# The second phase's order comes from twenty search passes with new prices, and the products by place load 128 columns

## The chip, the cores and the metric

The kernel runs on one core of a Trainium2 chip, as one launch. The metric is the time of one execution on the device in microseconds (us); three executions of the kernel before took 1140.48 to 1142.51 us, median 1141.89. A core has a matrix engine (PE, with its weight loads shown apart as PEld), a vector engine (DVE), an activation engine (ACT), a third elementwise engine (POOL), and SP, which here only issues transfers. Each engine works through its own list of instructions in the order in which they were written, and waits for the others at semaphores.

## The reference

Three layers follow one another. The kernel computes all of them, on 2304 tokens of 512 numbers:

```python
# 1. attention, 4 x 8 heads, 576 rows of 64: only the 32 largest scores of a row are kept
scores = scale * np.matmul(q, k.transpose(0, 1, 3, 2))
kth = np.partition(scores, -top_k, axis=-1)[..., -top_k:-top_k + 1]
scores = np.where(scores >= kth, scores, -1000000000.0)
attn = np.exp(scores - np.max(scores, axis=-1, keepdims=True))
x = (attn / (np.sum(attn, axis=-1, keepdims=True) + 1e-09)) @ v      # -> 2304 x 512
# 2. a dense layer, 512 -> 2048 -> 512
h = x @ w_in
x = np.where(h >= 1, h, np.where(h <= -1, 0.0, (h + 1) ** 2 / 4)) @ w_out
# 3. eight experts; each token goes to one, each expert takes 288 tokens at most
order = np.argsort(-(x @ w_gate).flatten())
for idx in order:                       # best pairs (token, expert) first
    tok, e = idx // E, idx % E
    if assigned[tok] < 0 and counts[e] < 288:
        assigned[tok] = e; counts[e] += 1
for e in range(8):
    out[assigned == e] = np.maximum(x[assigned == e] @ w1[e], 0) @ w2[e]
```

## The kernel before, in words

The program has two phases. The first does attention and the dense layer in blocks of 256 tokens; its last dense block is left half done for the second phase. The second phase does the rest of that block, the routing and the eight experts. This change touches the second phase alone.

No instruction is issued where it is written. Every call of an engine is recorded by a helper (`_Recorder.rec`, which is why nearly all rows of the profile name one line, L267, and are told apart by their tiles), with a price in nanoseconds, the tiles it reads and writes, and a rank. At the end of a phase `Program.issue` puts the recorded steps of all engines into one order and writes them out. `_pass` is a list scheduler: it plays the five engines through time and gives each engine, whenever it is free, the ready step with the smallest key. In pass 0 the key is the rank, which the author of the kernel wrote by hand (10 for each expert, with offsets such as `R_EX` and `R_XP`). Each further pass plays the steps backwards from their ends and takes the starts found there as new keys. `issue` keeps the order whose modelled end is earliest. Before, the first phase makes 10 further passes (`ROUNDS`), the second none (`ROUNDS_R = 0`): its order is the one by hand-written ranks.

What the second phase is made of, with the names that rows and order pieces use:

- **Routing** (`route`), eight rounds, one for each expert that fills up. Each has three search steps on DVE and PE: DVE writes `I` (128 x 2304 comparisons, in halves of 10 and 8 blocks), PE sums them into `pQ` by 18 small bf16 products (`pQ<-C,I`), DVE makes `ge`, PE spreads it (`pPT<-ge`), DVE takes `n0` and the next `y`, `yb`. From the third step come the expert's number `ei` and the tokens taken, counted through `SC` and a product into `pS` (`pS<-SC`).
- **Places** (`places`): DVE writes `oh`, a one-hot row of 96 for each token, and PE multiplies it by `Bt` in 18 small bf16 products (`pS<-Bt,oh`, weights `oh`); DVE reads off `idx`, the token numbers of the expert's 288 rows.
- **Gather** (`gathers`): three indirect transfers by POOL bring the rows `xg` out of `x2d` (the layer-2 output in DRAM).
- **The last dense block** (`last_block`): 96 products of 512 columns into `pX0` and `pX1`, copied by ACT into `yo` and stored to `x2d` by SP (`dram_x<-yo`); its rows for expert 0 are added by products with `taken` (`pH<-s,yo` and so on). The stores overwrite zero rows that the first gather reads, so they wait for it.
- **Expert** (`expert`): SP reads `ei` into a register and fetches eight pieces of the expert's weights, 512 KB each, into four buffers `raw` (four of w1, then four of w2). ACT rounds each to `W` (1024 columns), DVE writes the rest to another `W`. PE transposes `xg`, ACT and DVE split the result into two `XB`, and 192 products of 288 columns follow, 96 into `pH0`/`pH1` and 96 into `pX0`/`pX1` (`pH<-XB,W`, `pX<-XB,W`). Then transposes, `yo`, and three indirect stores by POOL. Since SP is one list, expert 0's w2 pieces stand behind the store `dram_x<-yo`.
- **Looks** (`look`, `totals`): 32 transfers of 512 KB into `s1`, each with two ACT passes (`size`), check the weights' range; `totals` turns them into a flag, read by all engines at the very end.

Of the kernel before, what the change touches and what calls it, by code (L numbers as in the profile page):

```python
# [11 lines left out]
BF16 = mybir.dt.bfloat16  # L12
# [28 lines left out]
R_QL, R_QS, R_QK, R_MK, R_PV, R_K, R_F, R_U = -4.0, -2.0, -1.2, 0.5, 1.0, 1.0, 1.5, 0.9  # L41
R_LB, SLOW, R_EX, R_XP, SPLIT_DVE, SPLIT_DVE0 = 12.0, 1.0, 25.0, -12.0, tuple(range(8)), tuple(range(8))
LATX, LATR, GRP = 1.5, 1.0, 1
ROUNDS, ROUNDS_R = 10, 0
X_DVE, H_DVE = True, tuple(range(8))
DEC0, GATE_H = 32, 0
WT_RAW, HALF, GD = False, 1.95, 1
# [165 lines left out]
class _Recorder:  # L213
# [5 lines left out]
    def __getattr__(self, method):  # L219
        def rec(*args, **kw):  # L220
            P, eng = self._prog, self._eng
            reads, writes = [], []
            for i, a in enumerate(args):
                if hasattr(a, "ap"):
                    (reads if i else writes).append(a)
            for k, a in kw.items():
                if hasattr(a, "ap"):
                    (writes if k in self.OUT else reads).append(a)
            if method == "matmul" and not kw["start"]:
                reads.append(writes[0])  # L230
            n = max(_free(a) for a in (writes[:1] if eng == "tensor" else reads + writes))
            inp = any(a.tensor.space == bass.MemoryType.PSUM for a in reads if hasattr(a.tensor, "space"))
            lat = None
            if eng == "vector":
                cost = 69 + 1.04 * n
                if method == "match_replace":
                    cost += 64
                if method == "tensor_scalar" and not inp:
                    cost = 69 + 0.52 * n
                if method == "scalar_tensor_tensor" and not inp:  # L240
                    cost = 69 + (1.04 if kw["in1"].dtype == I32 else 1.2) * n
                if method in ("tensor_tensor", "tensor_copy") and all(
                        x.dtype == BF16 and list(x.ap)[-1][0] == 1 for x in reads + writes):
                    cost = 69 + 0.52 * n
            elif eng == "scalar":
                cost = (51 if inp else 187) + 0.833 * n
                if not inp and args[2] in (AF.Copy, AF.Abs):
                    cost -= 93
                if "accum_out" in kw:
                    cost += 93  # L250
            elif eng == "gpsimd":
                cost = 148 + 2.1 * n
            elif eng == "sync":
                cost = max(60, 128 * min(_free(a) for a in reads + writes) * 4 / 360.0)
                lat = 2000 + 128 * min(_free(a) for a in reads + writes) * 4 / 180.0
            elif method == "transpose":
                cost = 109
            else:
                f32 = args[1].dtype == F32
                if args[1].dtype == F32R:  # L260
                    cost = 10 + 0.43 * n
                else:
                    cost = 2 * max(107, n * 2 / 2.4) + 1 if f32 else max(36, n / 2.4 + 3, 0.5 * _free(args[1]))
                if f32 and args[1].shape[-1] <= 64:
                    cost *= 0.63
            fn = getattr(getattr(P.nc, eng), method)
            P.add(eng, lambda: fn(*args, **kw), cost, reads, writes, lat)  # L267
        return rec


def _free(ap):
    n = 1
    for x in list(ap.shape)[1:]:
        n *= x
    return n
# [3 lines left out]
def kernel(ctx: ExitStack, tc: tile.TileContext, qm, qt, kT, vm, vt,  # L279
# [7 lines left out]
    pS = psum.tile([128, 2, 512], F32, name="pS")  # L287
# [8 lines left out]
    x2d = dram.tile([N, DM], F32, name="dram_x2")  # L296
# [550 lines left out]
    def second_phase(exact, rctx):  # L847
        rpool = rctx.enter_context(tc.tile_pool(name="rpool" + "x" * exact, bufs=1))
        P = Program(nc, LATR, True)
        V, A, G, T, Y = P.vector, P.scalar, P.gpsimd, P.tensor, P.sync  # L850
# [12 lines left out]
        def rt(shape, dt, tag, bufs=2):  # L863
            if tag not in rings:
                rings[tag] = Ring(tag, bufs, shape, dt)
            return rings[tag]()

        if exact:
# [3 lines left out]
            views, n = const_views(c1[:, 576:])  # L872
# [313 lines left out]
        def places(ph, ei, pos):  # L1186
            g1 = rt([128, NT], F32, "g1")
            V.tensor_scalar(g1, pos, 96.5, None, op0=ALU.is_ge)
            gq = rt([128, NT], BF16, "gq")
            V.scalar_tensor_tensor(out=gq, in0=pos, scalar=192.5, in1=g1, op0=ALU.is_ge, op1=ALU.add)  # L1190
            rr = rt([128, NT, 8], BF16, "rr8")
            V.scalar_tensor_tensor(out=rr, in0=bc(gq, [128, NT, 8], 2), scalar=-96.0, in1=bc(pos, [128, NT, 8], 2),
                                   op0=ALU.mult, op1=ALU.add)
            Bm = rt([128, 3, NT], BF16, "Bm")
            V.tensor_tensor(out=Bm, in0=bc(gq, [128, 3, NT], 1), in1=third, op=ALU.is_equal)
            Bt = rt([128, 2, 3, NT], BF16, "Bt")
            V.tensor_tensor(out=Bt, in0=bc(Bm, [128, 2, 3, NT], 1), in1=bc(tokb, [128, 2, 3, NT], 2), op=ALU.mult)
            for x, (ta, tb) in enumerate(HT):
                oh = rt([128, tb - ta, 96], BF16, f"oh{x}", 1)
                V.tensor_tensor(out=oh.rearrange("p t (g x) -> p t g x", x=8),  # L1200
                                in0=bc(rr[:, ta:tb], [128, tb - ta, 12, 8], 2),
                                in1=numbers(place96, tb - ta), op=ALU.is_equal)
                with P.group():
                    for t in range(ta, tb):
                        T.matmul(pS[:96, 1, :6], oh[:, t - ta, :], Bt.rearrange("p a g t -> p (a g) t")[:, :, t],
                                 start=(t == 0), stop=(t == NT - 1))
            idx = rt([96, 3], I32, "idx", 4)
            V.tensor_reduce(out=idx, in_=pS[:96, 1, :6].rearrange("p (a g) -> p g a", a=2), axis=AX, op=ALU.add)
            RES[ph] = (ei, idx)
# [31 lines left out]
        def gathers(ph):  # L1241
            idx = RES[ph][1]
            xg = XG[ph] = rt([96, 3, DM], F32, "xg", 2)

            def gather(g):
                return nc.gpsimd.indirect_dma_start(out=xg[:, g, :], out_offset=None, in_=x2d[:, :],  # L1246
                                                    in_offset=bass.IndirectOffsetOnAxis(ap=idx[:, g:g + 1], axis=0))

            P.rank -= 3.0
            for g in range(3):  # L1250
                P.add("gpsimd", partial(gather, g), 1000, [idx[:, g:g + 1], x2d[:, :]], [xg[:, g, :]], 3000)
            P.rank += 3.0

        def expert(ph):
            ei, idx = RES[ph]
            xg = XG[ph]
# [15 lines left out]
            hi, lo = [], []  # L1272
            for i in range(8):
                raw = rt([128, 1024], F32, "raw", 3 if exact else 4)
                P.add("sync", partial(fetch, raw, i // 4, i % 4), 1450, [ei[0:1, 0:1]] + [xg] * (early and i > 3), [raw], 2500)
                if i % 2 == 0:
                    wh, wl = W[wat[0] % 12], W[(wat[0] + 1) % 12]
                    wat[0] += 2
# [177 lines left out]
```

## Time and profile before

| | before |
|---|---|
| median of 3 executions | 1141.89 us |
| profiled execution, whole | 1138.19 us |
| profiled execution, first to last instruction (span) | 1136.3 us |
| PE busy in the span | 1051.2 us (93%) |
| DVE, ACT, POOL busy | 925.3, 808.9, 697.8 us |

The profiled execution is one run with the hardware profiler on; its own time is 1.9 us more than its span, and 3.7 us less than the median of the unprofiled ones. In the rows below, times are microseconds from the start of the span. In a timeline row, the numbers are start and length, and the brackets at its end say how long the engine stood idle before it and who released it. PEclk is the granted clock of PE: 1.00 is 2.4 GHz, 0.50 is 1.2 GHz.

### The profile page before, as it was taken

The numbers are of one execution on the slowest core, as the hardware profiler recorded it, in microseconds if no ns is written. First come the engines' busy times: TensorE is split into PE (matmuls) and PEld (weight loads), VectorE is DVE, ScalarE is ACT, GpSimd is POOL, SyncE is SP. The second block draws the span as 40 slices with busy tenths as digits, with TensorE's granted clock in tenths as the row PEclk, the third lists the DMA queues.
The fourth block names the chain that finished last, engine by engine and source line by source line (L and its number), as shares of the span: only waits on it lengthen the run. The fifth ranks groups of instructions, "written<-read, shape, count | busy, mean of one in ns | idle before, by whom it ended". The sixth has DMA issues, their size and how long they took to land.

```text
span 1136.3 us, 24504 instructions
## 1 busy us (share of the span) xinstructions
PE 1051.2 (93%) x8376; PEld 945.7 (83%) x8376; DVE 925.3 (81%) x2924; ACT 808.9 (71%) x1899; POOL 697.8 (61%) x880
## 2 busy tenths in 40 slices
PE   2777699999999989999999999999997999999995
PEld 1665588898888979898888888898976999999995
DVE  7899999899999899979889999984367987765430
ACT  4677787878888888967888888874305666666651
POOL 6988989977887887757697778773201132224111
PEclk9997799999999999999999999999988999999998
DMA  9744342441311442322243221212327687678720
GB/s 263 228 138 148 121 140 86 122 147 51 107 45 55 131 136 75 104 70 68 65 127 98 92 71 54 82 59 65 130 80 258 224 265 249 228 263 262 248 78 24
DMA packets 65783, 149.34 MB, mean 131 GB/s; under 512 B 15472, under 2 KB 23920, under 8 KB 65648
## 3 DMA queue, kind: packets, MB, share of 16 engines
q1 hardware_dynamic: 62576, 138.25, 38.1%
q0 software_dynamic: 3072, 9.44, 2.5%
q8 instruction: 67, 1.10, 0.4%
q14 instruction: 68, 0.56, 0.2%
HBM read 133.50 MB, written 14.16 MB: 130 GB/s over the span
## 4 chain that ended last, share of the span: by engine, by line
PE 57%; DVE 14%; issue 9%; ACT 7%; DMA 5%; POOL 4%; SPq 0%; POOLq 0%; ACTq 0%; DVEq 0%
PE pH L267 19%; PE pX L267 19%; PE pQ L267 7%; PE pS L267 7%; DVE f L267 5%; DVE m L267 4%; PE pPT L267 4%; ACT s L267 2%; DMA raw<-in_w_dram 2%; DMA s<-in_w_out_dram 2%; DVE pH L267 1%; DVE stage L267 1%; POOL s L267 1%; POOL out_dram L1340 1%; ACT W L267 1%
## 5 line engine op out<-in xcount | busy, mean ns | idle before, releaser
L267 PE MATMUL pH<-XB,W 128*128 128x256 f32 (+1 forms) x2496 | 366.8, 294 | 2.5 <-DVE XB L267 2.3
L267 PEld LDWEIGHTS pH<-XB,W 128*128 128x128 f32 x2496 | 331.0, 192 | 10.8 <-DVE XB L267 3.6
L267 DVE MAX8 m<-f 128x8 f32<-128x288 f32 x720 | 302.3, 448 | 3.5 <-POOL f L267 1.2
L267 POOL TENSOR_TENSOR s<-s,f 128x576 f32<-128x576 f32 x144 | 203.9, 1429 | 31.1 <-ACT f L267 28.2
L267 DVE MATCH_REPLACE8 f<-m,f 128x288 f32<-128x288 f32 x432 | 190.2, 443 | 0.1
L267 PE MATMUL pX<-W,XB 128*128 128x512 f32 x608 | 184.7, 410 | 0.3 <-ACT XB L267 0.2
L267 PE MATMUL pS<-XB 128*128 128x288 f32 (+2 forms) x672 | 145.5, 325 | 42.0 <-DVE f L267 18.7
L267 PEld LDWEIGHTS pS<-XB 128*128 128x128 f32 x672 | 107.2, 201 | 66.0 <-DVE f L267 25.1
L267 POOL TENSOR_TENSOR XB<-stage,XB 128x512 fp32r<-128x512 f32 (+1 forms) x96 | 127.1, 1325 | 55.3 <-ACT XB L267 36.4
L267 ACT ACTIVATE s<-s,sm 128x576 f32<-128x576 f32 x144 | 111.6, 776 | 25.4 <-POOL s L267 24.6
L267 PEld LDWEIGHTS pX<-W,XB 128*128 128x128 f32 x608 | 108.1, 192 | 18.1 <-issue 2.4
L267 ACT ACTIVATE s<-pS 128x576 f32<-128x576 f32 x144 | 92.9, 645 | 28.2 <-PE pS L267 27.5
L267 DVE TENSOR_TENSOR f<-pS,s 128x288 f32<-128x288 f32 x198 | 86.4, 448 | 30.7 <-ACT s L267 11.8
L267 PE MATMUL pX<-XB,W 128*128 128x288 f32 x768 | 109.9, 298 | 0.0
L267 ACT ACTIVATE f<-s,t_all 128x576 f32<-128x576 f32 x144 | 107.7, 773 | 2.5
L1246 POOL DMA_INDIRECT xg<-dram_x,idx x24 | 35.1, 1461 | 119.2 <-DVE idx L267 90.6
L267 PEld LDWEIGHTS pX<-XB,W 128*128 128x128 f32 x768 | 103.7, 188 | 0.2 <-issue 0.2
L267 DVE TENSOR_TENSOR W<-raw,W 128x1024 fp32r<-128x1024 f32 x64 | 76.7, 1219 | 33.2 <-ACT W L267 33.2
L267 PE MATMUL pPT<-ident,s 128*128 128x128 f32 x576 | 91.9, 284 | 8.3 <-ACT s L267 8.1
L1340 POOL DMA_INDIRECT out_dram<-yo,idx x24 | 26.8, 1116 | 115.3 <-ACT yo L267 110.9
L267 ACT ACTIVATE s<-pPT 128x512 f32<-128x512 f32 x144 | 85.1, 591 | 10.2 <-PE pPT L267 9.8
L267 ACT ACTIVATE W<-raw 128x1024 fp32r<-128x1024 f32 x64 | 65.3, 1054 | 35.7 <-DMA raw<-in_w_dram 33.1
(206 smaller groups left out, 1941.4 us busy)
## 6 DMA issues: line engine op xcount, KB each, us to landing
wl<-dram_wlo SPq DMA_DIRECT2D x64, 512.0 KB, 3.4
raw<-in_w_dram SPq DMA_DIRECT2D x64, 512.0 KB, 5.6
s<-in_w_in_dram SPq DMA_DIRECT2D x18, 512.0 KB, 6.0
s<-in_w_out_dram SPq DMA_DIRECT2D x18, 512.0 KB, 5.5
qr<-in_qm_dram SPq DMA_DIRECT2D x128, 64.0 KB, 2.3
stage<-in_w_in_dram SPq DMA_DIRECT2D x14, 512.0 KB, 4.4
stage<-in_w_out_dram SPq DMA_DIRECT2D x14, 512.0 KB, 3.5
stage<-in_kT_dram SPq DMA_DIRECT2D x48, 144.0 KB, 2.9
```

The lines of the kernel that those rows point to most:

```text
L267: P.add(eng, lambda: fn(*args, **kw), cost, reads, writes, lat)
L1246: return nc.gpsimd.indirect_dma_start(out=xg[:, g, :], out_offset=None, in_=x2d[:, :], in_offset=bass.IndirectOffsetOnAxis(ap=idx[:, g:g + ...
L1340: st = nc.gpsimd.indirect_dma_start(out=out, out_offset=bass.IndirectOffsetOnAxis(ap=idx[:, g:g + 1], axis=0), in_=yo, in_offset=None)
```

## The change

Three edits, all of them felt only where the second phase's steps are put in order, and one of them also in what is computed:

- `ROUNDS_R` goes from 0 to 20: the second phase's order is the one with the earliest modelled end out of 21 passes.
- Three prices that the search uses change: a bf16 product with 128 weight columns from 36 to 25 ns (others from 36 or more to 45), an indirect gather from 1000 to 1500 ns, a weight fetch from 1450 to 2000 ns.
- The 18 products by place take 128 columns of the flat one-hot tile in place of 96: the 96 of their own token block and the first 32 of the next. The extra 32 result rows are not read; the tile has 32 more columns, set to zero once.

```diff
-ROUNDS, ROUNDS_R = 10, 0
+ROUNDS, ROUNDS_R = 10, 20
...
-                    cost = 2 * max(107, n * 2 / 2.4) + 1 if f32 else max(36, n / 2.4 + 3, 0.5 * _free(args[1]))
+                    cost = 2 * max(107, n * 2 / 2.4) + 1 if f32 else max(25 if _free(args[1]) == 128 else 45, n / 2.4 + 3)
...
             for x, (ta, tb) in enumerate(HT):
-                oh = rt([128, tb - ta, 96], BF16, f"oh{x}", 1)
-                V.tensor_tensor(out=oh.rearrange("p t (g x) -> p t g x", x=8),
+
+                flat = rt([128, 96 * (tb - ta) + 32], BF16, f"oh{x}", 1)
+                if ph == 0:
+                    V.memset(flat[:, 96 * (tb - ta):], 0.0)
+                V.tensor_tensor(out=flat[:, :96 * (tb - ta)].rearrange("p (t g x) -> p t g x", x=8, g=12),
                                 in0=bc(rr[:, ta:tb], [128, tb - ta, 12, 8], 2),
                                 in1=numbers(place96, tb - ta), op=ALU.is_equal)
                 with P.group():
                     for t in range(ta, tb):
-                        T.matmul(pS[:96, 1, :6], oh[:, t - ta, :], Bt.rearrange("p a g t -> p (a g) t")[:, :, t],
+                        T.matmul(pS[:, 1, :6], flat[:, 96 * (t - ta):][:, :128], Bt.rearrange("p a g t -> p (a g) t")[:, :, t],
                                  start=(t == 0), stop=(t == NT - 1))
...
-                P.add("gpsimd", partial(gather, g), 1000, [idx[:, g:g + 1], x2d[:, :]], [xg[:, g, :]], 3000)
+                P.add("gpsimd", partial(gather, g), 1500, [idx[:, g:g + 1], x2d[:, :]], [xg[:, g, :]], 3000)
...
-                P.add("sync", partial(fetch, raw, i // 4, i % 4), 1450, [ei[0:1, 0:1]] + [xg] * (early and i > 3), [raw], 2500)
+                P.add("sync", partial(fetch, raw, i // 4, i % 4), 2000, [ei[0:1, 0:1]] + [xg] * (early and i > 3), [raw], 2500)
```

The first phase's order is the same word for word. In the second phase all five engines' orders differ. Three places of it follow, all at its start.

DVE, from the second half of `oh` for expert 0 to the first weight piece (`W1<-raw_0`), with `idx_0` among them. Before:

```order
L267 TENSOR_TENSOR oh1_0_9807<-rr8_0_9800,s0_105 128x768
L267 TENSOR_SCALAR y_1_9771<-mr_1_9763,bound_1_9767,iw_1_9769 128x18
L267 TENSOR_TENSOR y_0_9770<-y_1_9771,pen_0_9751 128x18
L267 COPY yb_1_9773<-y_0_9770 128x144
L267 TENSOR_TENSOR I0_0_9774<-yb_1_9773,s0_105 128x1280
L267 TENSOR_REDUCE idx_0_9808<-pS_66 96x3
L267 TENSOR_TENSOR I1_0_9775<-yb_1_9773,s0_105 128x1024
L267 TENSOR_TENSOR W1_92<-raw_0_9817,W0_91 128x1024
L267 TENSOR_SCALAR ge_1_9777<-pQ_68 128x8
```

Now:

```order
L267 TENSOR_TENSOR oh1_0_9807<-rr8_0_9800,s0_105 128x768
L267 TENSOR_REDUCE n0_1_9779<-pPT_67 128x1
L267 TENSOR_SCALAR y_1_9771<-y_0_9770,n0_1_9779 128x18
L267 COPY yb_0_9772<-y_1_9771 128x144
L267 TENSOR_TENSOR I0_0_9774<-yb_0_9772,s0_105 128x1280
L267 TENSOR_TENSOR I1_0_9775<-yb_0_9772,s0_105 128x1024
L267 TENSOR_REDUCE idx_0_9808<-pS_66 96x3
L267 TENSOR_TENSOR W1_92<-raw_0_9817,W0_91 128x1024
L267 TENSOR_SCALAR ge_0_9776<-pQ_68 128x8
```

What moved: before, `idx_0` stands behind the first half of `I` of route 1's first search step; now that whole step (its `I0` and `I1` stand above this piece, ahead of `oh`) and the `I0` and `I1` of the second step are ahead of `idx_0`.

ACT, from the second copy of the last dense block (`yo_1`) to expert 0's four input pieces (`XB<-pH0`, `pH1`, `pS`, `pX0`). Before:

```order
L267 ACTIVATE yo_1_9815<-pX1_72 128x512
L267 ACTIVATE size_0_9821,sizes_112<-s1_106 128x512
L267 ACTIVATE size_0_9821,sizes_112<-size_0_9821 128x512
L267 ACTIVATE W4_95<-raw_0_9817 128x1024
L267 ACTIVATE W4_95<-raw_1_9818 128x1024
L267 ACTIVATE W6_97<-raw_2_9819 128x1024
L267 ACTIVATE XB_103<-pH0_69 128x288
L267 ACTIVATE XB_103<-pH1_70 128x288
L267 ACTIVATE XB_103<-pS_66 128x288
L267 ACTIVATE XB_103<-pX0_71 128x288
```

Now (between `yo_1` and this piece stand the last three w1 pieces and a look):

```order
L267 ACTIVATE size_0_9821,sizes_112<-s1_106 128x512
L267 ACTIVATE size_0_9821,sizes_112<-size_0_9821 128x512
L267 ACTIVATE W4_95<-raw_0_9817 128x1024
L267 ACTIVATE XB_103<-pH0_69 128x288
L267 ACTIVATE XB_103<-pH1_70 128x288
L267 ACTIVATE W4_95<-raw_1_9818 128x1024
L267 ACTIVATE XB_103<-pS_66 128x288
L267 ACTIVATE XB_103<-pX0_71 128x288
```

What moved: the input pieces stood behind three of expert 0's w2 pieces (`W4`, `W4`, `W6`); now two of them stand behind one, the other two behind two.

SP, the first fetches of expert 0 (`raw`) and the first looks (`s1<-in_w_in`). Before:

```order
L1261 TENSOR_LOAD ei_0_9789
L1261 ISA x2
L1268 ISA
L1268 DMA raw_0_9817<-in_w1_dram 128x1024
L1268 ISA
L1268 DMA raw_1_9818<-in_w1_dram 128x1024
L1268 ISA
L1268 DMA raw_2_9819<-in_w1_dram 128x1024
L1268 ISA
L1268 DMA raw_3_9820<-in_w1_dram 128x1024
L267 DMA s1_106<-in_w_in_dram 128x1024
L267 DMA dram_x2_82<-yo_0_9814 128x512
```

Now:

```order
L1271 DMA raw_0_9817<-in_w1_dram 128x1024
L267 DMA s1_106<-in_w_in_dram 128x1024
L1271 ISA
L1271 DMA raw_1_9818<-in_w1_dram 128x1024
L1271 ISA
L1271 DMA raw_2_9819<-in_w1_dram 128x1024
L1271 ISA
L1271 DMA raw_3_9820<-in_w1_dram 128x1024
L267 DMA s1_106<-in_w_in_dram 128x1024
L267 DMA dram_x2_82<-yo_0_9814 128x512
```

What moved: a look has come in behind the first fetch; the store `dram_x2<-yo_0`, which waits for the gather, still stands ahead of the w2 fetches.

Elsewhere, on PE, the 18 products of a search step now mostly stand as 10 and 8 with other products between; the first search step of route 2 stands around expert 0's first three products, where 66 of them stood ahead of it; and `totals`, which stood in the middle of expert 7, stands behind its last product, ahead of the last transposes.

## Rows read from the trace of the kernel before

**Rows 1.** The page: busy time of PE and its granted clock in 40 slices.

```profile
PE 1051.2 (93%) x8376; PEld 945.7 (83%) x8376; DVE 925.3 (81%) x2924; ACT 808.9 (71%) x1899; POOL 697.8 (61%) x880
...
PEclk9997799999999999999999999999988999999998
```

**Rows 2.** Windows: stretch, length, busy us of each engine, granted clock, DMA share.

```profile
854.00:861.00 7.00, 5.96 (x41) 4.87 (x41) 5.44 (x10) 4.57 (x8) 3.02 (x2) 1.00 0.58 204
...
865.00:868.60 3.60, 2.50 (x11) 1.54 (x9) 2.34 (x3) 1.67 (x2) 0.00 (x0) 1.00 1.03 368
868.60:872.80 4.20, 0.13 (x2) 0.01 (x1) 3.14 (x17) 3.69 (x7) 0.00 (x0) 0.91 0.43 172
872.80:879.00 6.20, 6.04 (x26) 5.94 (x27) 4.90 (x17) 1.28 (x5) 0.00 (x0) 0.51 0.71 246
...
890.00:1000.00 110.00, 108.03 (x1015) 104.11 (x1014) 90.37 (x255) 71.02 (x154) 29.95 (x31) 1.00 0.72 239
1000.00:1124.50 124.50, 122.63 (x997) 120.15 (x997) 57.42 (x126) 71.85 (x156) 22.28 (x30) 1.00 0.55 182
```

**Rows 3.** Timeline, start of the second phase: start, length, engine, instruction, idle before.

```profile
851.74 0.15 DVE L267 TENSOR_REDUCE idx<-pS 96x3 int32<-96x6 f32 x1
...
859.84 0.46 PE L267 MATMUL pH<-ident,xg 96*128 96x96 f32 x2 [0.81 <-DMA xg<-dram_x,idx]
...
859.95 0.33 SPq L267 DMA_DIRECT2D dram_x<-yo  x1
...
860.55 1.64 SPq L1269 DMA_DIRECT2D raw<-in_w_dram  x3
...
864.56 1.06 ACT L267 ACTIVATE W<-raw 128x1024 fp32r<-128x1024 f32 x1 [3.91 <-DMA raw<-in_w_dram]
...
866.47 1.06 ACT L267 ACTIVATE W<-raw 128x1024 fp32r<-128x1024 f32 x1 [0.86 <-DMA raw<-in_w_dram]
...
869.06 1.06 ACT L267 ACTIVATE W<-raw 128x1024 fp32r<-128x1024 f32 x1 [1.53 <-DMA raw<-in_w_dram]
870.02 0.69 ACT L267 ACTIVATE XB<-pH 128x288 fp32r<-128x288 f32 x2
...
872.65 0.80 DVE L267 TENSOR_TENSOR XB<-pH,XB 128x288 fp32r<-128x288 f32 x2
...
872.80 0.19 PE L267 MATMUL pS<-SC,s 128*128 128x1 bf16 x1 [4.07 <-DVE SC L267]
...
873.14 6.01 PE L267 MATMUL pH<-XB,W 128*128 128x288 f32 x24 [0.16 <-DVE XB L267]
```

**Rows 4.** Timeline, the same stretch: DVE's steps of one search step, PE's last block.

```profile
854.26 4.36 PE L267 MATMUL pX<-W,XB 128*128 128x512 f32 x18
...
856.70 0.23 DVE L267 COPY yb<-y 128x144 bf16<-128x144 bf16 x1
...
858.06 1.42 DVE L267 TENSOR_TENSOR I<-yb,s 128x1280 bf16<-128x1280 bf16 x2
...
865.64 1.23 DVE L267 TENSOR_TENSOR W<-raw,W 128x1024 fp32r<-128x1024 f32 x1 [1.41 <-ACT W L267]
```

**Rows 5.** Chain that ended last, in order of time: one search step's and one place's products.

```profile
843.87 0.46 PE pQ L267 x18
...
957.83 0.79 PE pS L267 x18
```

**Rows 6.** Timeline of PE in the steady part: two of its stalls.

```profile
913.90 0.35 PE L267 MATMUL pQ<-C,I 128*128 128x8 bf16 x8 [0.18 <-DVE I L267]
...
1021.39 1.86 PE L267 MATMUL pH<-XB,W 128*128 128x288 f32 x12 [0.99 <-DVE XB L267]
```

**Rows 7.** Timeline: a small DVE memset, and PE's last transposes.

```profile
829.54 0.07 DVE L267 MEMSET closed<- 128x8 f32 x1 [0.17 <-POOL XB L267]
...
1124.33 0.64 PE L267 MATMUL pS<-ident,s 128*96 128x128 f32 x4 [0.24 <-ACT yo L267]
```

**Rows 8.** The page, DMA issues: KB each, median us from issue to landing.

```profile
s<-in_w_out_dram SPq DMA_DIRECT2D x18, 512.0 KB, 5.5
```

## The prediction

> **What bounds the kernel now.** I read the page first, then windows over the second phase, then the timeline where the windows show PE idle. The reader is to see in the busy shares that PE is the bound: 93% of the span, and the slices of its clock show low ones at the start and at the change of phase, about three quarters along [rows 1]. The first phase keeps its order, so only what lies behind about 829 us can change, where the second phase's memsets stand [rows 7]. There the windows matter: from 890 to 1124.5 us PE is busy 108.03 of 110 and 122.63 of 124.5 us [rows 2]. That leaves 1.97 + 1.87 = 3.8 us to be won by any order over seven and a half experts. The rest of the idle time sits where expert 0 starts: 1.0 us in 854 to 861, 1.1 us in 865 to 868.6, 4.1 us in 868.6 to 872.8, and then 6.2 us at a granted clock of 0.51, close to the lower of its two levels, 1.2 GHz [rows 2]. At half speed these 6.2 us do the work of about 3.1, so the low clock costs 3.0.
>
> The timeline says why expert 0 starts late. `idx` is there at 851.74, the gather lands at 859.84, the store to DRAM that waits for it goes at 859.95, the w2 fetches behind it at 860.55, and ACT takes three of these pieces at 864.56, 866.47 and 869.06 before it comes to the `XB` pieces at 870.02. DVE follows at 872.65, and PE, 4.07 us idle, starts on expert 0 at 873.14 [rows 3]. So a step that needs the gather alone waits for three weight transfers because of its place in ACT's list.
>
> **The change part by part.** *The places.* Expert by expert, 18 products go from 96 to 128 weight columns. In the chain 18 place products took 0.79 us, and 18 search products, which have 128 columns of the same type and 8 result columns in place of 6, took 0.46 [rows 5]. If the places become like the search, each expert saves 0.33 us of PE. Places of expert 1 and later lie in the stretch where PE is the bound, so seven count: 7 x 0.33 = 2.3 us. The bounds are 0 (the width alone does nothing) and 8 x 0.33 = 2.6. I take 2.3, since the row of the search products is the nearest there is. More columns could also cost: a load in proportion to its columns would make 0.79 into 0.79 x 128/96 = 1.05, a loss of 8 x 0.26 = 2.1 us; the search products, 128 wide at 0.46, speak against it.
>
> The Trainium skill has both rules, on the page "TensorE: Matmul & The Clock Gate". Its section "LDWEIGHTS (loading the stationary operand)" lets a load grow with the number of columns, which would go against this change. Its section "Weight-path perf modes — Fast Weight Load (FWL) and DoubleRow" has a faster load switch on where there are exactly 128 weights and the type isn't FP32, which 96 columns miss. Rows 5 side with the second; by the first alone the sum below would be worse by 2.3 + 2.1 = 4.4 us.
>
> *Expert 0's start.* Two moves work against each other. On DVE `idx` falls behind: it now has two whole pairs of `I` ahead of it (1.42 each) where it had the larger half of one (1280 of 2304 columns, about 0.8), and one more `y` and `yb` (0.23 each at the row of `yb`), so 2 x 1.42 - 0.8 + 0.46 = 2.5 us [rows 4]. Besides, PE has five more products of the last block ahead of route 0's last count, at 4.36 / 18 = 0.24 each, 1.2 us [rows 4]. So `idx` comes about 3.7 us later, at 855.4. Gather, store and first w2 fetch are the same chain as before, 864.56 - 851.74 = 12.8 us from `idx` to ACT's start on the piece [rows 3]: 868.2 now. Against this, the first two `XB` stand behind one piece (1.06) and not three: ACT is through them at 868.2 + 1.06 + 0.69 = 870.0, almost when it began them before (870.02). DVE has one weight piece in between (1.23 us from 869.3, when ACT has finished it) and then half of the 0.80, so the first product of expert 0 can go at about 870.9 [rows 3, 4]. I add half a microsecond for waits that I can't place: 871.5, against 873.14, a gain of 1.6. The third and fourth `XB` stand behind the second piece, which comes 1.9 us after the first [rows 3], and reach PE about 1.5 us after the first two, while nine products of the ready half run.
>
> PE meanwhile has done route 2's first 18 search products (0.46), which stood inside expert 0. Gain here 1.6 + 0.5 = 2.1; I take 2.0. Below, the bound is that the 3.7 us of `idx` come through whole (rival four); above, that PE idles no more than it must, the whole 4.07 saved [rows 3]. A look more between expert 0's first and second fetch delays w1 pieces, but their cover is the gather: they are due only with the first product, at 871.5. If that cover goes, the start moves by the time of one transfer, 1.9 us at the spacing of the w2 pieces.
>
> PE is idle longer in all before that point, since it runs out of the last block at about 858.6 (854.26 + 4.36) [rows 4] and the gather lands near 863.5. I therefore let the clock fall as it did: before, it fell right after the 4.07 us in which PE stood still [rows 2, 3]. Gain 0, with 3.0 if it stays up.
>
> *The steady part.* Splitting the 18 search products into 10 and 8 with other work between removes waits for the second half of `I`, such as the 0.18 before the eight at 913.90 [rows 6]. There is one search step after the other, but only some of them wait; I count three such waits, 0.6 us. The larger kind, PE waiting 0.99 for `XB` at 1021.39 [rows 6], has the same causes as before (an in-order ACT that waits for a transfer), and I leave it as it is. Bounds: all of the 3.8 us gained, or as much again lost.
>
> *Small things.* The two new memsets (0.07 at the like row) lie on DVE ahead of route 0, under the wait for PE's transposes; without that cover 0.14 us [rows 7]. `totals` now stands ahead of PE's last transposes. It needs the last look, whose transfer lands 5.5 us after issue [rows 8]. In ACT's new list three copies of `pX` stand between the last two looks, so at least 48 products, 7.4 us at 1.86 for 12 [rows 6]: enough for the transfer. So I price it at 0; a look that comes a whole transfer late would move the transposes (1124.33) [rows 7] and the stores behind them by up to 5.5 us. Its place on SP and POOL changes nothing that is waited for: the gather for expert 2 now stands behind the stores of expert 0, but has most of expert 1 to land in.
>
> **Sum.** 2.3 + 2.0 + 0.6 = 4.9 us. The profiled execution took 1138.19 us, so 1133.3 by it. It lies 3.7 under the median of the runs without a profile, 1141.89, on which the forecast is made: 1137.0.
>
> **Rivals.** *One: it gains much more.* If the reordered start leaves PE idle in short pieces, the low clock (3.0) doesn't come, and the start gains near 3.5: 2.3 + 3.5 + 0.6 + 3.0 = 9.4, 1132.5 us. For it: the work is there to fill. Against it: PE needs the gather, and nothing else is left to do from 858.6 to its landing.
>
> *Two: it comes out even.* The later `idx` eats the start's gain and steady waits grow by as much as the places save in part: 2.3 - 1.0 = 1.3, 1140.6. For it: 98% of the steady part is PE already.
>
> *Three: the places don't do what is meant,* and the wide loads cost by their columns: -2.1 + 2.0 + 0.6 = 0.5 gained, 1141.4. Only rows 5 can tell, and speak against.
>
> *Four: slower.* `idx` 3.7 us later carries the store, the w2 fetches and ACT's and DVE's lists with it, and the shorter list ahead of `XB` doesn't help, because transfers land later among more looks. Then expert 0 starts at 873.14 + 3.7 = 876.8, PE is idle in two long pieces and the clock is low in two stretches, one of them new (3.0): -3.7 - 3.0 + 0.5 + 2.3 + 0.6 = -3.3, 1145.2. It decides as soon as expert 0's first product falls behind about 877.
>
> **How the numbers follow.** The forecast 0.52, one 0.15, two 0.16, three 0.04, four 0.13. A change of less than 0.2%, 2.3 us, can't be told from none. The forecast's own range is 1134.3 to 1139.5, nearly all of it faster; with rival one that makes 0.66 faster. Two and three, and the forecast's edge, make 0.22 the same, and four, cut a little for its nearer outcomes, 0.12 slower. For 8 in 10 the range reaches to a part of rival one and past two: 1131.3 to 1142.8.
>
> **What would show it.** Right: 18 place products in about 0.46 us; expert 0's first product between 870.5 and 872.5 and `idx` between 854.5 and 856.5; a low clock near 872; PE's last transposes between 1117 and 1122 where they were at 1124.33 [rows 7]; PE idle of 3 to 4 us between 890 and there. Wrong: place products still at 0.79, a start at 877, several stalls near 1 us in the steady part, or a wait before the last transposes.

## The result, and the profile after

The changed kernel takes 1128.27 us (median of 6 runs, 1125.24 to 1130.77), the kernel before in the same set of runs 1139.41 (6 runs, 1135.29 to 1142.51). The ratio is 0.9911, 95% interval 0.989 to 0.9931: 10.1 us by the ratio, 11.1 by the two medians, twice the 4.9 us that were forecast, and outside the range. The profiled execution took 1128.89 us with a span of 1127.1 (before: 1138.19 and 1136.3).

The page of the profile after has the same busy share of PE as before, 93%, and its clock's low slices are nearly where they were, at the start and about three quarters along [rows 1]:

```profile
PE 1047.0 (93%) x8376; PEld 940.8 (83%) x8376; DVE 924.2 (82%) x2926; ACT 810.1 (72%) x1899; POOL 696.5 (62%) x880
...
PEclk9987799999999999999999999999988999999998
```

The windows answer to [rows 2] (stretch, length, busy us of PE, PE's loads, DVE, ACT and POOL, PE's granted clock, DMA share and GB/s):

```profile
854.00:861.00 7.00, 6.27 (x59) 4.08 (x57) 5.37 (x16) 2.24 (x4) 2.44 (x3) 1.00 0.95 339
861.00:865.00 4.00, 2.24 (x24) 1.82 (x25) 3.67 (x10) 3.97 (x7) 1.12 (x1) 0.72 0.81 221
865.00:868.60 3.60, 3.60 (x14) 3.03 (x14) 3.60 (x18) 1.64 (x5) 0.00 (x0) 0.50 0.90 281
868.60:872.80 4.20, 4.20 (x17) 3.44 (x15) 3.19 (x13) 1.47 (x2) 0.00 (x0) 0.50 0.84 232
872.80:879.00 6.20, 6.20 (x67) 5.47 (x67) 5.16 (x11) 3.07 (x8) 0.00 (x0) 0.99 0.79 310
890.00:1000.00 110.00, 109.98 (x1053) 107.00 (x1052) 91.69 (x258) 74.14 (x152) 31.10 (x31) 1.00 0.77 254
1000.00:1115.00 115.00, 114.14 (x930) 112.47 (x929) 54.57 (x119) 69.49 (x156) 21.16 (x30) 1.00 0.58 189
```

Two things are to be seen. PE's idle time in the steady part is nearly gone (0.02 us in 110, 0.86 in 115). And the low clock, 0.50, the lower of the two levels (1.2 GHz), now begins between 861 and 865 us (0.72) and lasts to about 872.8, under the transposes ahead of expert 0, and is over when expert 0 runs; before it lay on expert 0's first products [rows 2].

The timeline of the same start answers to [rows 3] (start, length, engine, instruction, idle before it and what ended that):

```profile
856.88 0.15 DVE L267 TENSOR_REDUCE idx<-pS 96x3 int32<-96x6 f32 x1
...
861.38 0.41 PE L267 MATMUL pQ<-C,I 128*128 128x8 bf16 x10 [1.11 <-DVE I L267]
...
861.98 0.35 PE L267 MATMUL pQ<-C,I 128*128 128x8 bf16 x8 [0.20 <-DVE I L267]
...
863.24 0.17 PE L267 MATMUL pPT<-ge,ones_f 128*128 128x8 bf16 x1 [0.90 <-DVE ge L267]
...
863.69 1.85 PE L267 MATMUL pH<-ident,xg 96*128 96x96 f32 x6 [0.28 <-DMA xg<-dram_x,idx]
...
864.89 0.33 SPq L267 DMA_DIRECT2D dram_x<-yo  x1
...
869.78 1.06 ACT L267 ACTIVATE W<-raw 128x1024 fp32r<-128x1024 f32 x1 [1.65 <-DMA raw<-in_w_dram]
...
872.24 0.41 ACT L267 ACTIVATE XB<-pH 128x288 fp32r<-128x288 f32 x1 [1.40 <-PE pH L267]
...
875.33 0.64 PE L267 MATMUL pH<-XB,W 128*128 128x288 f32 x3
```

The long wait of 4.07 us is gone; ahead of the transposes stand four short ones, 1.11, 0.20, 0.90 and 0.28 us. Yet expert 0 starts later: PE goes through the transposes at half speed, ACT's first `XB` waits for them, and from 865 to 879 us PE itself has no idle time at all.

**Where the 9.2 us between the two spans came from.** I cut both traces at three points: the last copy of the logits `L` (829.21 us before, 830.73 after), expert 0's first product (873.14, 875.33) and the last expert product (1122.54, 1113.08). From the start to `L`: +1.5 us. Its order is the same; over all profiles here `L` comes between 826.3 and 832.9, so traces are compared from `L` on. From `L` to expert 0: 43.94 to 44.59, +0.65. From expert 0 to the last product: 249.39 to 237.75, **-11.64**. Behind it: +0.26. So the experts' stretch gave all of it.

In that stretch I took the distance from each product's start to the next one's, less the usual distance of its kind (133 ns for expert products). What exceeds 110 ns I call a stall: 21 of them before, 7.1 us in all, and 3 after, 1.1 us. That is 6.05 of the 11.64. The half clock inside the stretch cost 2.65 before and nothing after. Place products went from 46 to 27 ns apart: 7 x 18 x 0.019 = 2.4 us. The three make 11.1 of the 11.64. The sum holds in every trace below: take stalls, half clock and, where places load 96 columns, 2.4 us off the stretch, and 236.4 to 237.9 are left. How the three share the gain is known for this pair of executions alone: e1 below, with the order of before, had no half clock in the stretch and more stalls.

One stall of before shows both the mechanism and why I had sized it too small (timeline of the kernel before, same columns; the product that waits is in [rows 6]):

```profile
1010.65 9.51 SPq L267 DMA_DIRECT2D s<-in_w_out_dram  x2
...
1019.04 0.66 ACT L267 ACTIVATE size<-s 128x512 f32<-128x512 f32 x1 [1.62 <-DMA s<-in_w_out_dram]
...
1019.36 1.03 PE L267 MATMUL pH<-XB,W 128*128 128x288 f32 x6
...
1020.45 0.69 ACT L267 ACTIVATE XB<-pH 128x288 fp32r<-128x288 f32 x2
...
1020.88 0.46 DVE L267 SCALAR_TENSOR_TENSOR XB<-pH,XB 128x288 fp32r<-128x288 f32 x1 [1.57 <-ACT XB L267]
```

A look's transfer is issued at 1010.65. ACT comes to read it, waits 1.62 us with an `XB` copy behind it, DVE waits for that copy, and PE for DVE. Six products that start at 1019.36 and stand 0.133 apart let the next one go near 1020.2; it goes at 1021.39. The loss is 1.15 us where the row shows 0.99, since the last product's modelled length (about 0.3 us) covers the first part of the wait, 0.16 us here. The stall at 913.90, where [rows 6] show 0.18, is 0.32 by the starts: nearly half is covered. Over a stretch the two kernels' waits of ACT show the same (view of waits, ACT, 880 to 1115 us: us in total, times, longest; first the kernel before, then the changed one):

```profile
ACT size L267 <- DMA s<-in_w_out_dram: 6.7, 5, 2.0
ACT size L267 <- DMA s<-in_w_in_dram: 5.1, 4, 2.1
...
ACT W L267 <- DMA raw<-in_w_dram: 2.7, 2, 2.5
```

```profile
ACT XB L267 <- PE pH L267: 39.1, 33, 2.6
ACT s L267 <- PE pX L267: 28.0, 18, 2.8
ACT W L267 <- DMA raw<-in_w_dram: 3.4, 5, 1.9
...
ACT size L267 <- DMA s<-in_w_out_dram: 0.2, 1, 0.2
```

Nine waits for looks, 11.8 us, stand in the first and one of 0.2 us in the second. PE's own waits, which are under-read as said, show what the prediction had left as it was (view of waits, PE, 880 to 1124 us in the kernel before, then 880 to 1115 in the changed one):

```profile
PE pH L267 <- DVE XB L267: 2.5, 5, 1.0
PE pQ L267 <- DVE I L267: 0.6, 3, 0.2
```

```profile
PE pH L267 <- DVE XB L267: 0.6, 1, 0.6
```

The one wait of 0.6 us that is left, a stall of 0.78 at 1004.04, has the same chain with a weight piece in place of a look: ACT stands 1.95 us at a piece, with the `XB` copy behind it.

### The profile page after: what moved, and what is told of

The parts are those of the page before. It is cut to its first block, busy times and chain, and to the rows that moved or that the text cites. A ratio compares the mean times of both kernels' runs of the same rounds, so it can differ in the third digit from the quotient of the medians.

```text
span 1127.1 us, 24499 instructions
## 1 busy us (share of the span) xinstructions
PE 1047.0 (93%) x8376; PEld 940.8 (83%) x8376; DVE 924.2 (82%) x2926; ACT 810.1 (72%) x1899; POOL 696.5 (62%) x880
## 4 chain that ended last, share of the span: by engine, by line
PE 65%; DVE 15%; ACT 5%; issue 5%; POOL 4%; DMA 2%; SPq 0%; POOLq 0%; DVEq 0%; ACTq 0%
PE pH L267 24%; PE pX L267 23%; PE pS L267 7%; PE pQ L267 7%; DVE f L267 5%; DVE m L267 5%; PE pPT L267 4%; ACT s L267 2%; DVE pH L267 2%; DVE stage L267 2%; POOL s L267 1%; POOL f L267 1%; POOL XB L267 1%; ACT stage L267 1%; DMA raw<-in_w_dram 1%
## 5 line engine op out<-in xcount | busy, mean ns | idle before, releaser
L267 PE MATMUL pX<-XB,W 128*128 128x288 f32 x768 | 113.7, 299 | 0.0
L267 ACT ACTIVATE s<-pPT 128x512 f32<-128x512 f32 x144 | 85.2, 592 | 10.2 <-PE pPT L267 9.8
L267 PE MATMUL pQ<-s,v 128*64 128x128 f32 (+1 forms) x1280 | 88.2, 283 | 2.3 <-ACT tr L267 1.8
```

## The experiments

All are timed against the kernel before, on the same chip. e1 to e4 ran on one chip, e5 and e7 to e9 on a second, e6 and e10 to e12 on a third, so medians compare within such a group and ratios across them. *Stalls* and *stretch* (expert 0's first product to the last expert product) are worked out from each trace as above, *start* is from `L` to expert 0's first product, *looks* is ACT's wait for looks from 880 to 1115 us; all in us.

| run | median | ratio to before, 95% | start | stretch | stalls | looks |
|---|---|---|---|---|---|---|
| before (profile) | | | 43.94 | 249.39 | 7.1 | 11.8 |
| after (profile) | 1128.27 | 0.9911 [0.989, 0.9931] | 44.59 | 237.75 | 1.1 | 0.2 |
| e1_places_alone | 1139.98 | 1.0013 [0.9993, 1.0032] | 44.04 | 249.76 | 12.0 | 11.6 |
| e2_search_old_prices | 1138.26 | 1.0001 [0.9983, 1.0018] | 39.95 | 253.39 | 10.7 | 11.3 |
| e3_prices_no_search | 1134.43 | 0.9978 [0.9964, 0.9991] | 44.24 | 244.30 | 6.7 | 0.5 |
| e4_new_order_96 | 1128.88 | 0.9934 [0.991, 0.9959] | 43.37 | 241.62 | 2.7 | 0.2 |
| e8_product_price_alone | 1131.18 | 0.9957 [0.9936, 0.9978] | 43.31 | 247.24 | 9.0 | 9.2 |
| e9_transfer_prices_alone | 1133.86 | 0.9969 [0.9945, 0.9993] | 42.16 | 246.50 | 8.1 | 3.8 |
| e7_after_clock_fillers | 1127.08 | 0.992 [0.9894, 0.9947] | 42.83 | 238.32 | 1.6 | 0 |
| e5_before_small_looks | 1132.46 | 0.9961 [0.9942, 0.998] | 44.61 | 243.30 | 4.0 | 0.2 |
| e6_after_small_looks | 1126.03 | 0.9892 [0.9873, 0.9912] | 43.79 | 236.54 | 0.1 | 0 |
| e10_looks_read_later | 1142.50 | 1.0035 [1.0022, 1.0048] | 45.08 | 253.80 | 12.0 | 8.1 |
| e11_more_fillers | 1125.04 | 0.9889 [0.987, 0.9908] | 42.64 | 238.39 | 1.6 | 0 |
| e12_two_passes | 1126.73 | 0.9902 [0.9885, 0.9919] | 45.45 | 237.58 | 0.9 | 0 |

Each trace is one execution, and not always a typical one (e4's took 1133.71 us, its median is 1128.88). The changed kernel's order gave starts of 44.59 and 45.45 (e12), so less than a microsecond of a single trace decides nothing.

**The parts of the change, one at a time.** Four runs: the 128 columns in the order of before; the search with the old prices; the new prices without the search; the new order with 96 columns.

```
e1  order of before; pS[:, 1, :6], flat[:, 96 * (t - ta):][:, :128]
e2  cost of products: max(36, n / 2.4 + 3, 0.5 * _free(args[1])); gather 1000; fetch 1450
e3  ROUNDS, ROUNDS_R = 10, 0
e4  order of after; pS[:96, 1, :6], flat[:, 96 * (t - ta):][:, :96]
```

> The second phase keeps the order of before step for step (two small memsets more); only the place products take 128 columns. Theory (the width is worth its pitch and no more, the rest of the gain is the order): 18 products fall from 0.79 to about 0.46 us, seven experts' worth counts, the kernel gains 2.0 to 2.6 us on before, and the stretch from expert 0's first product to expert 7's last falls from 249.4 to about 247. Rival (width makes the gain, since earlier place numbers also end waits of DVE and of the gather behind it): 6 us or more of the 10. Rival (PE waits there anyway): under 0.5 us.

> Twenty search passes and 128 columns, but the gather, fetch and bf16 prices of before. Theory (the search takes the waits out of PE's list, the prices only trim it): 7 to 10 us faster than before, the stretch from expert 0's first product to expert 7's last near 239 us, PE waits there a few tenths in number. Rival (the search is only as good as its prices: with fetches at 1450 it packs transfers too tightly and the waits stay): 2 to 4 us faster, stretch near 245.

> The new prices and 128 columns, but no search pass: the order is the one by hand-written ranks, played with the new prices. Theory (search): 2 to 4 us faster than before, mainly the place products; PE's waits inside the experts stay, stretch from expert 0's first product to expert 7's last near 246 us. Rival (prices): 7 us or more faster, stretch below 241.

> The order of the changed kernel step for step, but the place products load 96 columns again. Theory: 2.3 us slower than the changed kernel, so about 8 us faster than before; 18 place products at about 0.79 us, the stretch from expert 0's first product to expert 7's last 237.8 + 2.3 = 240.1. Rival (in the new order the width is hidden behind other waits): same as the changed kernel within 0.5 us.

e1 won nothing, though its place products do stand 27 ns apart and no half clock lies in its stretch: its stalls are 12.0 us against 7.1, which takes back the 2.4 us of the places and the 2.65 of the clock. e2 won nothing either: its expert 0 starts 4 us earlier, and the stretch gives it back with 10.7 us of stalls and 4.9 of half clock. e3 won 0.2%, e4 0.66%. So the order carries most of the gain, and it takes the search and the prices together. By the traces the width is worth something only there: 241.62 against 237.75 in the stretch, of which 2.4 are the products themselves. By the medians it is 0.23% (0.9934 against 0.9911), and the intervals overlap, so the times alone don't show it. The chain of waits has the same place of one expert in both (start, length, engine, tile, products; first 96 columns in e4, then 128 in the changed kernel):

```profile
925.88 0.79 PE pS L267 x18
```

```profile
924.04 0.48 PE pS L267 x18
```

**Which price.** e8 keeps the new price for bf16 products alone, e9 those of fetches and gathers alone.

```
e8  gather 1000; fetch 1450
e9  cost of products: max(36, n / 2.4 + 3, 0.5 * _free(args[1]))
```

> Twenty passes and 128 columns as in the changed kernel, with the new price for bf16 products alone; fetches stay at 1450 ns and gathers at 1000 ns. Theory: with the old price of 64 ns the planner thinks that the searches' and places' products (504 of them, measured 27 ns apart) fill TensorE, so that it sees no wait worth moving anything for; by its own account the search wins 0.5 us with the old prices, and 5.7 us with this price. So most of the gain is here: 1128 to 1131 us, stalls beyond 110 ns between expert products of under 3 us (7.1 before, 1.1 after). Rival: the transfers' prices are what lets it issue fetches early enough; then this lands at 1135 to 1140 us, with stalls of 6 us or more.

> Twenty passes and 128 columns, with the new prices of fetches (2000 ns) and gathers (1500 ns), and the old price of bf16 products. Theory (the product price carries the gain): 1135 to 1140 us, stalls between expert products of 6 us or more. Rival (the transfers' prices carry it): 1128 to 1132 us, stalls of under 3 us.

The old price of a product with 128 weight columns is 0.5 x 128 = 64 ns, by the formula of e9, and not 36 as the list of the change has it; so the new price, 25, is a cut by more than half. Neither theory held. e8 came to 1131.18, just above what it expected, but with 9.0 us of stalls, not under 3; e9 lies between the two. Each set of prices brings a part (0.43% and 0.31%), and the two together 0.9 to 1.0%, no less than their sum. With the product price alone ACT again waits for transfers, 9.7 us for weight pieces and 9.2 for looks; that the planner, by its low prices of transfers, takes them to be there is likely, but no run shows it (waits of ACT in e8, same columns):

```profile
ACT W L267 <- DMA raw<-in_w_dram: 9.7, 9, 2.7
ACT size L267 <- DMA s<-in_w_in_dram: 8.4, 4, 2.9
...
ACT size L267 <- DMA s<-in_w_out_dram: 0.8, 1, 0.8
```

**The passes.** `ROUNDS, ROUNDS_R = 10, 2`.

> The changed kernel with two passes in place of twenty: by the planner's own account its best order is that of the second pass (end 285.4 us for the order by ranks, 279.8 after one pass, 278.4 after two, 278.6 in all later ones), so the instructions and their order are those of the changed kernel on every engine. Expected 1127 to 1130 us; it is also the changed kernel's time on the chip of the other three runs.

As expected. In its trace every engine does the same steps in the same order as in the changed kernel's, so eighteen of the twenty passes change nothing, and it is also a second measurement of the changed kernel.

**The looks.** Is it the transfers that looks make, or where they stand? All looks but the first are cut to 64 columns, in either order; and in e10 ACT reads each look later in the order of before.

```
+        def peek(raw, n):
+            w = 1024 if n == 0 else 64
+            return nc.sync.dma_start(out=raw[:, :w], in_=words_of(n).bitcast(I32)[:, :w])
```

> The kernel before, in the same order, with 31 of the 32 looks transferring 64 of their 1024 columns (32 KB in place of 512 KB); most of the weights' range check is left out. Theory (the order itself leaves the waits): 1136 to 1139 us, stalls between expert products 5 us or more. Rival: the waits come from the looks' transfers, beside which fetches land late, and the new order is only better at keeping them apart: then 4 to 7 us are won here, 1132 to 1135 us, with stalls of under 3 us.

> The changed kernel, in its own order, with 31 of the 32 looks transferring 64 of their 1024 columns; most of the weights' range check is left out. Between 880 and 1115 us ScalarE waits 11.8 us for looks' transfers in the kernel before and not at all in the changed one. Theory (those waits of ScalarE's in-order queue are what the new order is rid of): nothing is left to win by small looks, 1126.5 to 1129 us, within 0.15% of the changed kernel, where the same edit won the kernel before 0.39%. Rival (looks cost by the bandwidth that they share with the fetches): the same 3 to 5 us are won here too, 1123 to 1125.5 us.

> The kernel before, all of it, with one thing moved: the two ScalarE instructions that read a look stand one or two of ScalarE's other instructions later, as far as the next look's transfer into the same tile leaves room; VectorE, TensorE, GpSimd and the DMA queues keep their order. Theory (ScalarE stands at a look's transfer with a copy behind it that TensorE's next products need): ScalarE's waits for looks between 880 and 1115 us fall from 11.8 to under 6 us and 1.5 to 4 us are won, 1134 to 1136.5 us. Rival (bandwidth or the queue of transfers): the transfers are the same, so the time is, 1137 to 1139 us. It could also lose 1 us where a look that is read later holds up the next look and the fetch behind it.

In the order of before small looks won 0.39%, the rival's size (its stalls are 4.0, though, not under 3); ACT's waits for them fell from 11.8 to 0.2 us and the stalls from 7.1 to 4.0, the one of 1.15 us at 1021.39 among those gone. In the new order they won about 0.1% (0.9892 against 0.9902 for the same program with whole looks on the same chip, intervals that overlap). The looks move as many bytes in either order, so it is where they stand that cost time; and ACT's waits for weight pieces are 2.7 us in e5 as in the kernel before, so the gain of e5 does not come from fetches that land earlier for ACT. By the stalls that is a third of the gain (3.1 of 9.2 us), by the medians some four tenths (0.39 of 0.89 to 0.98%); the other 4 us of stalls stand in e5 and are gone in e6.

e10 fell: it lost 0.35% where it was to win. The waits moved (ACT in e10):

```profile
ACT W L277 <- DMA raw<-in_w_dram: 6.8, 2, 3.4
ACT size L277 <- DMA s<-in_w_in_dram: 4.4, 2, 3.7
ACT size L277 <- DMA s<-in_w_out_dram: 3.7, 3, 1.8
```

All looks go through one tile, so a look that is read later lets the next look, and the fetches behind it on SP, go later. That fits the waits for weight pieces, which rose from 2.7 to 6.8 us, while those for looks fell only to 8.1. So the test of ACT's place alone failed, and e5 and e6 are what bears on the looks. In the order of before the look of 1010.65 stands behind the four w2 fetches of its expert, and ACT got it 8.4 us after its issue; in the new order a look stands between the first and the last two w2 fetches of the same expert (SP's issues, first before, then changed):

```profile
1004.91 5.18 SPq L1269 DMA_DIRECT2D raw<-in_w_dram  x4
1010.65 9.51 SPq L267 DMA_DIRECT2D s<-in_w_out_dram  x2
```

```profile
1004.16 0.35 SPq L267 DMA_DIRECT2D s<-in_w_in_dram  x1
1004.76 1.43 SPq L1272 DMA_DIRECT2D raw<-in_w_dram  x2
```

**The clock.** Products that nothing reads, in the waits ahead of expert 0: 7 in e7, 12 in e11.

```
+        def keep_busy(n):
+            for _ in range(n):
+                P.ops[-1]["calls"].append(partial(nc.tensor.matmul, pH[0], g8[7][:, 0][:, 0, :128],
+                                                  wout_hi[3][:, :DM], start=True, stop=True))
...
e7   keep_busy(4) behind the last block, (3) behind the search products that follow
e11  keep_busy(5) behind the last block, (1) and (4) behind those products' halves, (2) behind their count
```

> The changed kernel with 7 products of 512 columns that nothing reads, put where TensorE waits ahead of expert 0: 4 behind the last product of the last block (a wait of 1.11 us follows there) and 3 behind the search products at 861.98 us (a wait of 0.90 us). All else stands in the same order. Theory: the half clock from 862.7 to 873.0 us comes because TensorE did little between 860 and 863.7 us, and it makes expert 0 start late: kept at full clock, expert 0's first product comes at 872 to 873.5 us in place of 875.33, and the kernel ends 2 to 3 us earlier, 1125 to 1126.5 us. Rival one: the clock stays up and the start is set by ScalarE's copies of the w2 pieces, whose transfers are as late as before: under 1 us is won. Rival two: 7 products are too few, the half clock comes all the same, and the time is the changed kernel's, 1128 us, or up to 1 us above.

> The changed kernel with 12 products of 512 columns that nothing reads, in place of the 7 of the run before: 5 behind the last block, 1 and 4 behind the two halves of the search products that follow, 2 ahead of the gathered rows' transposes. With 7 the half clock there fell from 10.3 to 3.4 us. Theory: with 12 it goes wholly, expert 0's first product comes 42.0 to 42.6 us behind the last logits (44.59 in the changed kernel, 42.83 with 7), and against the changed kernel on the same chip 1.5 to 2.5 us are won. Rival: the products that are added lie on the path themselves (0.24 us each, where the gaps are 0.2 to 0.5 us), or expert 0 waits for its w2 pieces: no more than 1 us is won.

Windows of e11 over the start (columns as above):

```profile
854.00:861.00 7.00, 7.00 (x62) 4.68 (x60) 5.19 (x13) 3.45 (x7) 3.55 (x3) 1.00 0.89 299
861.00:864.00 3.00, 2.66 (x16) 2.04 (x16) 2.97 (x16) 1.37 (x2) 0.00 (x0) 1.00 0.76 250
864.00:870.00 6.00, 5.44 (x38) 4.08 (x37) 5.90 (x20) 4.09 (x9) 0.00 (x0) 1.00 0.87 294
```

The granted clock stays at 1.00, the higher level, where it was 0.50 from 865 to 872.8 in the changed kernel. Expert 0 starts 42.64 us behind `L`, against 44.59 and 45.45 in the two profiles of the changed kernel, so 2.0 to 2.8 us earlier; the stretch gives back 0.6 to 0.8. By the medians on one chip 1125.04 against 1126.73, 1.7 us. The intervals of the two ratios overlap, so the time alone doesn't settle it; the clock and the start in the trace speak for it. Over the six runs of each the mean granted clock is 0.968 in e11 and 0.964 in e12, though single runs overlap (0.962 to 0.970 and 0.959 to 0.969). With 7 fillers (e7) part of the half clock was left, and the start was 42.83; its time alone can't be told from the changed kernel's. e11 has the lowest median of the versions that leave nothing out; its interval overlaps the changed kernel's.

## Why the prediction was wrong, point by point

**The base.** The forecast, 1137.0, lies 8.7 us above the result. 2.5 of them are its base: it was made from three runs of the kernel before with the median 1141.89, and six gave 1139.41. The other 6.2 are the gain, 11.1 in place of 4.9.

**The step that failed** is the steady part. The prediction counted three waits, 0.6 us (they are there, PE's three waits for `I`, and gone), and said of the larger kind, PE waiting for `XB` at 1021.39: it "has the same causes as before (an in-order ACT that waits for a transfer), and I leave it as it is". The cause was right. That it would stay was not: PE's waits for `XB` fell from 2.5 to 0.6 us, ACT's for looks from 11.8 to 0.2, and the stalls, counted by the starts, by 6.05. So a term of 0.6 measured some 6.

**Its bound was wrong too.** "3.8 us to be won by any order" came from PE's busy time, in which each wait is covered in part by the product before it. By start to start there were 7.1 us of stalls and 2.65 of half clock behind expert 0's start. The next column of [rows 2] was nearer: PE's loads were busy 104.11 of 110 and 120.15 of 124.5 us, so idle 5.9 + 4.3 = 10.2, and after it is 3.0 + 2.5 = 5.5. The Trainium skill says so on the page "Perfetto Trace Analysis", section "Identifying the Most-Contended Engine": matmul busy share misleads for TensorE because its instructions are pipelined, and the busy share of the weight loads is one of the two measures to take instead. This trace agrees that it misleads: the idle time of the loads fell by 4.7 us, that of the products by 2.96 (3.84 to 0.88). The page's reason is that pipelined instructions look smaller in the trace; here they looked longer, about 0.29 us at 0.133 from start to start.

**The places**, 2.3 us: mechanism and size were right, 0.79 became 0.48 [rows 5], 2.4 us in the new order. But e1 shows that the term is no saving by itself: in the order of before it won nothing. The bound "0, the width alone does nothing" stood there for another reason than the one that holds, for the loads did get shorter, from 126 to 96 ns (groups of loads in 880 to 1120 us before and in 880 to 1110 in the changed kernel; after the bar busy us and mean ns):

```profile
L267 PEld LDWEIGHTS <-oh 128*96 128x96 bf16 x108 | 6.0, 126 | 0.4 <-DVE oh L267 0.3
```

```profile
L267 PEld LDWEIGHTS <-oh 128*128 128x128 bf16 x108 | 3.5, 96 | 0.7
```

Of the two rules of the Trainium skill that were weighed, the one in "Weight-path perf modes — Fast Weight Load (FWL) and DoubleRow" of the page "TensorE: Matmul & The Clock Gate", a faster load where there are 128 weights and the type isn't FP32, agrees with these rows, and with 27 in place of 46 ns between products in e1 and the changed kernel.

**Expert 0's start**, 2.0: nothing was gained, +0.65 in the profile, where the order of before alone spreads from 43.94 to 44.61 (e5). `idx` came 26.15 us behind `L`, 22.53 before: 3.6 later, as forecast (3.7). ACT took its weight piece when the sum had it, too: 869.78, against 868.2 and the 1.5 us by which `L` itself came later. What failed is the next step: ACT could not go on to its `XB` pieces but waited 1.40 us until 872.24, and not for want of the shorter list. It waited for PE's transposes at half speed, which the sum had at no cost. Nor had ACT's list been all of the wait before: its first two `XB` copies were through at 870.71, and DVE came to them at 872.65 [rows 3], behind a weight piece (870.15) and twelve small steps of the search. With the clock kept up (e11) the start is 1.3 us earlier than before's.

**The low clock**, 0: the prediction let it fall as it had, "right after" the 4.07 us; by the 0.91 of 868.6 to 872.8 [rows 2] it fell within them, some 0.8 us (0.09 x 4.2 / 0.5) before their end. In the changed kernel it fell 9 us earlier, ahead of the transposes. There it ate the start's gain, and expert 0 kept full speed: 2.65 us less in the stretch of this pair of profiles. e1 and e5, in the order of before, had their half clock there as well (about 863 to 873), so this placing is not shown to be the new order's doing, and the profile of before from which the prediction was read is the odd one of three.

**Small things**, 0: right, though the 48 products that were to cover the last look are 6.4 us by the starts (48 x 0.133), not 7.4. The totals' products stand ahead of PE's last transposes without a wait, and these come at 1114.87, 2.1 us earlier than the earliest that the prediction named.

Rival one had the size, 9.4 us, for a wrong reason (3.0 of clock and 3.5 of start). What stays open is which moves removed the 4 us of stalls that small looks leave in the order of before. In the traces of before and e5 PE waits at several of them for DVE (`I`, `XB`, `ge`), so moves of DVE's steps are likely; no run here moved them one by one.

## What to carry to other kernels

Size waits on TensorE by start to start, or by the busy share of its loads, and not by the busy share of its products. A scheduler's search is worth what its prices are worth: with the old ones it found nothing here, with new ones near the measured times 0.7% more than the same prices without it. A saving on the engine that is the bound can be lost where a wait stands ready to take its place, as the places' was in e1. And one profile of a kernel isn't its order: look at a second execution before pricing where the clock falls.

## What the runs showed of the hardware

Bf16 products with 128 weight columns and 6 result columns follow each other every 27 ns, with 96 weight columns every 46 ns. Products that do nothing, put into the short waits of a stretch, changed TensorE's half clock there: in the one trace of each, 7 left part of it, 12 left none, and the transposes then ran at full speed. One look's transfer of 512 KB behind four others was read by ACT 8.4 us after its issue, where the median to landing is 5.5 [rows 8].
